# Retention and routed experts on one core: logits one chunk further behind, expert 0's weights loaded later and evenly, and a third list for expert 0

## The chip, the core and the metric

The kernel runs on one core of a Trainium2 chip. Its engines are TensorE (PE, with its weight loads shown apart as PEld), VectorE (DVE), ScalarE (ACT), GpSimd (POOL) and SyncE (SP); each takes its own instructions in the order in which they are written. SP issues most transfers, POOL the gathers and scatters, and 16 DMA engines carry them all. TensorE's clock is granted at one of two levels, 1.2 or 2.4 GHz (0.50 and 1.00 in the rows). The metric is the time of one execution on the device in microseconds (us), the median of several.

## The reference

Four sequences of 768 tokens with 8 heads of 64 run through a linear attention with decay ("retention"); its output, 3072 tokens of 512 numbers, goes through a layer of 8 experts of which each token uses the two with the largest noisy logits.

```python
for t in range(S):
    state = gamma[None, :, None, None] * state + np.einsum('bhd,bhe->bhde', k[:, :, t], v[:, :, t])
    y[:, :, t] = scale * np.einsum('bhd,bhde->bhe', q[:, :, t], state)
...
logits = x @ w_gate
noise_scale = np.log1p(np.exp(x @ w_noise))
noisy_logits = logits + noise_scale * noise
top2 = np.argpartition(-noisy_logits, 2, axis=1)[:, :2]
...
h = np.maximum(x[mask] @ w1[e], 0.0)
out[mask] += top2_w[mask, k, None] * (h @ w2[e])
```

## The kernel before

**Retention** goes through 24 chunks of 128 tokens, six to a sequence. `qk(j)` makes chunk j's first product (16 matmuls, L306, always the first of its chunk in the trace) and DVE masks it into `am` (L309). `y_mm(j)` makes the chunk's output `pY` (L316, L320) and, except in a sequence's last chunk, the state's increment `pU` (L324), which ACT copies into `U` (L330) for the next chunk's L316; the first chunk of a sequence reads no `U`. Then ACT squares `pY` for its norm (L333), DVE makes the scale (`x_scale`, L152 to L155), ACT makes `xs` and its float16 half (L342, L343), POOL the rest (L344), and SP sends the result twice: transposed to `xt` for the logits (L346) and to `xbuf` in memory for the experts (L347). `logits(j)` (L353, L356) are 8 small matmuls on `xt`.

The loop at L633 writes these in a fixed order. Iteration j holds `qk(j+1)`, the scaling of v and q on POOL, `x_scale(j-1)` and `x_split(j-1)`, the loads of chunk j+4, `y_mm(j)`, the logits of an earlier chunk, and then what a table `todo[j]` names. So on DVE an iteration is the mask of chunk j+1, the scale of chunk j-1 and the table's work; on ACT `xs` and its half come before `U`.

**Routing** of a sequence b is such table work, in steps: `route_a` (logits out of PSUM), `route_b` (the two largest, one-hot), `route_c` (exponential on ACT, weights; on PE the places in the lists, L404 and L407), `route_h`, `route_d` (places), `route_e` twice (one-hot matrices `ob`, `a`, `bb`, L468 to L478), `route_f` (12 matmuls, L485, added to `acc`), `route_g`. The tuple `when` gives the iteration of each, counted from the sequence's last chunk.

**Experts.** A token list per expert is packed into blocks of 128 slots. Expert 0 is worked on first, and its first 384 slots (list 0, the first two sequences) already while the last sequence is routed: `units` are eight `mm1` (first product of 384 slots, L672 to L674, 12 matmuls each) and three `mm2` (second product of a block, L702 to L704), and `early(n)` puts n of them into PE's order. Its other tokens (list 8) begin at slot 384 or later. `slots` reads a block's tokens from `acc`, `gather` fetches them (POOL, L591), `x_t` transposes them into `xe` (SP, L598), `put` scatters the result (POOL, L693). The weights of expert 0 come in quarters by `w_load` (SP, L171), `w_sum` (ACT, L175), `w_hi` (ACT, L192) and `w_lo` (DVE, L197), from the same table; those of expert 1 are loaded after the ranking of the experts, and the rest follow one expert ahead. The order after the loop is written out by hand:

```python
    early(1)
    logits(NCH - 3)
...
    early(1)
    logits(NCH - 2)
...
    early(1)
    logits(NCH - 1)
    route_a(b)
    route_b(b)
```

Of the kernel before, what the change touches and what calls it, by code (L numbers as in the profile page):

```python
# [32 lines left out]
# fullest with the most slots.  What exceeds an expert's slots goes through the loop at the end.  # L33
B0 = B // 2
FIRST = 384
NL = E + 1
NBLK, CAP = 7, 832
CAPS = [832, 832, 816, 800, 800, 784, 768, 768]      # expert 0, then by rank
NCOL = NBLK * E
BASE = [NBLK * 128 * e for e in range(E)] + [0]  # L40
NV = 5
BIG = 1.0e6
# powers of two that the float16 parts are scaled to (bounds of the norms)
# [4 lines left out]
for _n, _w in (("ident", 128), ("mask", 128), ("tri", 128), ("lanes", 128), ("blks", NCOL),  # L48
               ("lidx", NL), ("base", NL), ("rcap", E - 1), ("tie", E - 1), ("tok1", NCH), ("tokv", NCH * 2), ("pad", 1), ("i64", 64),
               ("vtab", NC * H), ("gtab", NC * HP)):  # L50
    _C[_n] = (_o, _o + _w)
    _o += _w
# [4 lines left out]
def _constants():  # L57
# [11 lines left out]
    put("lidx", np.arange(NL)[None, :])  # L69
    put("base", np.array(BASE)[None, :])  # L70
# [21 lines left out]
def moe_kernel(ctx, tc, qT, kT, kt, vt, noise, wgn, w1, w2, ctab, qtab, xbuf, out):  # L92
# [9 lines left out]
    # keeps the tensor engine's clock up while the first operands come in  # L102
# [28 lines left out]
    idx = consts.tile([128, NCOL], I32, name="idx")            # by rank  # L131
# [12 lines left out]
    LST = pR[:, 160:160 + NV * NCOL].rearrange("p (v n) -> p v n", v=NV)  # L144
    SUM = pR[:, 480:488]

    def pow2(ss, target, up, down):
        """Power of two that brings a vector with sum of squares ss below 2^target, and its inverse."""
        # sqrt(ss) < 2^(m - 62) with m half the biased exponent of ss; powers of two by their bits
# [13 lines left out]
    def w_load(e, which, i, n=1):  # L163
        # n quarters from the ith on
# [44 lines left out]
    # ================= retention and routing =================  # L209
# [33 lines left out]
    def zero_out(i):  # L243
        # the output and the rows of padding start as zeros
# [44 lines left out]
    def q_table(c):  # L289
        # the decay of chunk c's queries, out of chunk 0's  # L290
# [84 lines left out]
    def route_b(b):  # L375
        # noisy logits, the two largest
        lg, sp = R[b]
        o = int(b >= B0)
        ny = work.tile([128, NC, NL], F32, name="ny")
        nc.vector.tensor_tensor(sp, sp, nz[:, b * NC:(b + 1) * NC, :], op=OP.mult)  # L380
        nc.vector.memset(ny[:, :, 0:1] if o else ny[:, :, E:NL], -3.0e38)
# [9 lines left out]
        for k in range(2):  # L391
            nc.vector.tensor_tensor(oh[:, k], K("lidx")[:, None, :].to_broadcast(s3),
                                    i8[:, :, k:k + 1].to_broadcast(s3), op=OP.is_equal)
# [6 lines left out]
    def route_c(b):  # L400
        # places in the lists
# [14 lines left out]
        # what the slots get: token + 1 in two parts, the weight in three, each exact in bfloat16  # L416
# [15 lines left out]
    def route_d(b):  # L432
# [11 lines left out]
        if b == B0 - 1:  # L444
            nc.vector.tensor_scalar(cn[:, E:NL], cn[:, 0:1], float(FIRST), None, op0=OP.max)
# [14 lines left out]
    def route_e(b, k):  # L460
        # the slots' tokens and weights as sums of one-hot products
# [10 lines left out]
        # the last sequence's are waited for: GpSimd takes a part  # L472
# [21 lines left out]
    def slots(n0, n1):  # L494
        # token + 1 and weight, 0 in empty slots
# [6 lines left out]
    def rows_of(tk, n0, n1):  # L502
        # the slots' rows in xbuf and out; a row of padding for an empty slot
# [4 lines left out]
    def ranks():  # L508
        # experts 1, ..., 7 by their tokens' number
# [8 lines left out]
        pm = hp.tile(s3, F32, name="pm")           # rank by expert  # L518
# [15 lines left out]
    def route_g(b):  # L534
        # what the loop over the places beyond the lists needs
# [10 lines left out]
    def loop_table():  # L546
        # blocks beyond the lists: how many, of which list, from which place
# [38 lines left out]
    def gather(e, t):  # L586
        o, n, i = block(e, t)
        if t == 0:
# [3 lines left out]
            out=x[:n], out_offset=None, in_=xbuf[:128 + B0 * S] if e == 0 and t < 3 else xbuf,  # L592
# [347 lines left out]
```

## Time and profile before

| | |
|---|---|
| median of 3 runs | 724.33 us (724.18 to 725.54) |
| profiled execution, first to last instruction | 733.5 us |
| TensorE busy | 685.0 us, 93% of the span |
| VectorE, ScalarE, GpSimd busy | 294.0, 311.0, 237.9 us |
| mean granted TensorE clock | 0.954 |

The page gives no time of the profiled execution but its span; that is 9.2 us above the median of the runs without a profile. PE's busy time is no measure of speed where the clock is at half, since the same matmul is then busy for longer.

### The profile page before, as it was taken

What the parts mean: (1) busy time and instruction counts of PE and PEld (TensorE: products, weight loads), DVE (VectorE), ACT (ScalarE), POOL (GpSimd) and SP (SyncE); (2) the same over time, 40 slices, a digit from 0 to 9 for tenths busy, and PEclk for the clock granted to TensorE, in tenths of its full rate; (3) what the DMA queues carried; (4) which work ended last, traced back from release to release, by engine and by line L of the source; (5) the groups of instructions that cost most, each with busy time, mean ns of one, the idle gap of its engine ahead of it and who ended that gap; (6) DMA issues with size and microseconds to landing.
All of it is one profiled execution on the core that took longest, in us unless ns stands there. A gap on an engine that the chain in (4) does not pass through costs nothing.

```text
span 733.5 us, 12009 instructions
## 1 busy us (share of the span) xinstructions
PE 685.0 (93%) x4789; PEld 431.0 (59%) x4789; DVE 294.0 (40%) x719; ACT 311.0 (42%) x562; POOL 237.9 (32%) x186
## 2 busy tenths in 40 slices
PE   8879879889879999999999999999999999999991
PEld 6879769777448555455546545654555466446540
DVE  3326778695942573215221521432152225216100
ACT  4554444447204374344443534443444435344110
POOL 4564734652333220431033123304321421240021
PEclk9997787986999999999999999999999999999997
DMA  9999955995869953467367826744673685353032
GB/s 331 260 296 245 290 181 165 294 294 146 303 115 248 216 163 130 88 115 221 84 115 120 267 45 119 182 155 86 116 218 85 122 177 185 68 104 60 11 47 30
DMA packets 116057, 119.09 MB, mean 162 GB/s; under 512 B 82560, under 2 KB 82816, under 8 KB 112416
## 3 DMA queue, kind: packets, MB, share of 16 engines
q1 hardware_dynamic: 104080, 91.25, 45.0%
q0 software_dynamic: 11344, 26.22, 19.4%
q10 hardware_dynamic: 576, 0.84, 0.4%
q8 instruction: 38, 0.62, 0.4%
q14 instruction: 19, 0.16, 0.1%
HBM read 72.67 MB, written 26.21 MB: 135 GB/s over the span
## 4 chain that ended last, share of the span: by engine, by line
PE 76%; DVE 8%; DMA 7%; ACT 3%; issue 2%; POOL 1%; SPq 1%; POOLq 0%; ACTq 0%
PE pH L672 11%; PE pH L673 11%; PE pH L674 11%; PE pO L702 10%; PE pO L704 10%; PE pO L703 10%; PE pY L320 3%; DMA xt<-x 3%; PE pA L306 2%; PE pY L316 2%; PE pU L324 1%; DMA wst<-w 1%; DVE am L309 1%; DVE bb L478 1%; DMA xe<-xg 1%
## 5 line engine op out<-in xcount | busy, mean ns | idle before, releaser
L693 POOL DMA_INDIRECT out<-ot,idx x54 | 84.9, 1573 | 360.2 <-ACT ot L688 214.4
L672 PE MATMUL pH<-xe,w1h 128*128 128x384 f16 (+4 forms) x544 | 176.6, 325 | 3.9 <-DMA xe<-xg 3.3
L673 PE MATMUL pH<-xe,w1h 128*128 128x384 f16 (+4 forms) x544 | 176.5, 324 | 0.0
L674 PE MATMUL pH<-xe,w1l 128*128 128x384 f16 (+4 forms) x544 | 176.4, 324 | 0.0
L676 DVE SCALAR_TENSOR_TENSOR hl<-pH,hh 128x384 f16<-128x384 f32 (+4 forms) x136 | 74.4, 549 | 210.5 <-ACT hh L675 209.7
L704 PE MATMUL pO<-w2h,hl 128*128 128x512 f16 x384 | 145.5, 379 | 0.0
L703 PE MATMUL pO<-w2l,hh 128*128 128x512 f16 x384 | 145.5, 379 | 0.0
L702 PE MATMUL pO<-w2h,hh 128*128 128x512 f16 x384 | 145.5, 379 | 0.0
L675 ACT ACTIVATE hh<-pH 128x384 f16<-128x384 f32 (+4 forms) x136 | 65.7, 483 | 127.1 <-PE pH L674 125.2
L688 ACT ACTIVATE ot<-pO,gse 128x512 f32<-128x512 f32 (+4 forms) x54 | 37.0, 686 | 173.8 <-PE pO L704 169.3
L197 DVE SCALAR_TENSOR_TENSOR w1l<-wst,wsc,w1h 128x1024 f16<-128x1024 f32 x32 | 42.7, 1339 | 106.8 <-ACT w1h L192 106.8
L672 PEld LDWEIGHTS <-w1h 128*128 128x128 f16 x544 | 54.2, 100 | 34.5 <-DMA xe<-xg 1.7
L673 PEld LDWEIGHTS <-w1h 128*128 128x128 f16 x544 | 53.5, 98 | 35.4 <-issue 2.8
L674 PEld LDWEIGHTS <-w1l 128*128 128x128 f16 x544 | 53.5, 98 | 34.5 <-issue 0.3
L175 ACT ACTIVATE junk<-wst 128x1024 bf16<-128x1024 f32 x64 | 67.1, 1049 | 5.6 <-DMA wst<-w 2.8
L704 PEld LDWEIGHTS <-hl 128*128 128x128 f16 x384 | 37.5, 98 | 45.8 <-DVE hl L676 0.5
L702 PEld LDWEIGHTS <-hh 128*128 128x128 f16 x384 | 38.1, 99 | 44.1
L703 PEld LDWEIGHTS <-hh 128*128 128x128 f16 x384 | 37.5, 98 | 44.2
L591 POOL DMA_INDIRECT xg<-xbuf,idx x54 | 54.7, 1014 | 25.9 <-issue 14.9
L320 PE MATMUL pY<-vp,am 128*128 128x64 f32 x384 | 60.4, 292 | 0.0
L320 PEld LDWEIGHTS pY<-vp,am 128*128 128x128 f32 x384 | 58.1, 220 | 0.6 <-issue 0.2
L344 POOL TENSOR_TENSOR x<-xs,x 128x512 f16<-128x512 f32 x23 | 32.3, 1405 | 58.6 <-issue 32.3
(163 smaller groups left out, 778.1 us busy)
## 6 DMA issues: line engine op xcount, KB each, us to landing
wst<-w SPq DMA_DIRECT2D x28, 1024.0 KB, 9.2
in_q<-qT SPq DMA_DIRECT2D x24, 256.0 KB, 3.7
in_k<-kT SPq DMA_DIRECT2D x24, 256.0 KB, 4.2
in_v<-vt SPq DMA_DIRECT2D x24, 256.0 KB, 4.9
in_kt<-kt SPq DMA_DIRECT2D x24, 256.0 KB, 5.0
xbuf<-x SPq DMA_DIRECT2D x24, 256.0 KB, 2.6
out<-zero SPq DMA_DIRECT2D x6, 1024.0 KB, 12.6
wst<-w SPq DMA_DIRECT2D x8, 512.0 KB, 7.6
```

Of the source, the lines that this page charges most:

```text
L175: nc.scalar.activation(junk, st[:, i * 1024:(i + 1) * 1024], AF.Square, accum_out=ss[:, i:i + 1])
L320: nc.tensor.matmul(pY[:, 2 * i + s, :], AM[j][:, s, i, :], VP[j][:, 2 * i + s, :], start=(not c and i == 0 and s == 0), stop=True, skip_gr ...
L591: nc.gpsimd.indirect_dma_start(out=x[:n], out_offset=None, in_=xbuf[:128 + B0 * S] if e == 0 and t < 3 else xbuf, in_offset=bass.IndirectO ...
L672: nc.tensor.matmul(p[:, :n], whi, xh, start=(k == 0), stop=False)
L673: nc.tensor.matmul(p[:, :n], whi, xl, start=False, stop=False)
L674: nc.tensor.matmul(p[:, :n], wlo, xh, start=False, stop=(k == KT - 1))
L675: nc.scalar.activation(hh[:, f, n0:n1], p[:, :n], AF.Relu)
L676: nc.vector.scalar_tensor_tensor(hl[:, f, n0:n1], p[:, :n], 0.0, hh[:, f, n0:n1], op0=OP.max, op1=OP.subtract)
L693: nc.gpsimd.indirect_dma_start(out=out, out_offset=bass.IndirectOffsetOnAxis(ap=idx[:n, i:i + 1], axis=0), in_=ot[:n], in_offset=None, com ...
L702: nc.tensor.matmul(p, a, WT["2h"][:, f, :], start=(f == 0), stop=False)
L703: nc.tensor.matmul(p, a, WT["2l"][:, f, :], start=False, stop=False)
L704: nc.tensor.matmul(p, c, WT["2h"][:, f, :], start=False, stop=(f == FT - 1))
```

## The change

Five things change; all else, the experts 1 to 7 included, is written in the same order.

1. `logits` stand three chunks behind instead of two, and `when` is moved with them: `route_b` and `route_c` no longer share an iteration, but `route_c` and `route_h` do, and so do `route_d` and the first `route_e`.
2. Expert 0's weights start two iterations later (w1) and are spread over every second iteration (w1 in 5 to 11, w2 in 13 to 19; before 3 to 9 and 17 to 20).
3. The third sequence's `route_f` moves from the last iteration to behind the first early unit; its second `route_e` moves into the last iteration.
4. The fourth sequence's tokens of expert 0 get a list of their own (list 9 of 10) that begins at slot 576 or later. So slots 384 to 575 are ready once the third sequence is routed: `units` gain eight `mm1` of 192 slots and a fourth `mm2`. Of the block that is cut at 576 the two halves are gathered and transposed apart.
5. `route_g` of the last two sequences and the loop's table move from expert 0's second product to expert 1's.

```diff
-    LST = pR[:, 160:160 + NV * NCOL].rearrange("p (v n) -> p v n", v=NV)
+    LST = pR[:, 168:168 + NV * NCOL].rearrange("p (v n) -> p v n", v=NV)
...
-            nc.vector.tensor_tensor(oh[:, k], K("lidx")[:, None, :].to_broadcast(s3),
+            nc.vector.tensor_tensor(oh[:, k], K("lidx3" if b == B - 1 else "lidx")[:, None, :].to_broadcast(s3),
...
-            nc.vector.tensor_scalar(cn[:, E:NL], cn[:, 0:1], float(FIRST), None, op0=OP.max)
+            nc.vector.tensor_scalar(cn[:, E:E + 1], cn[:, 0:1], float(FIRST), None, op0=OP.max)
+        if b == B - 2:
+            nc.vector.tensor_scalar(cn[:, E + 1:NL], cn[:, E:E + 1], float(SECOND), None, op0=OP.max)
...
-        when = (1, 2, 2, 3, 3, 4, 5, 6, 7) if b < B - 2 else (1, 2, 2, 3, 3, 3, 4, 5)
+        when = (2, 3, 4, 4, 5, 5, 6, 7, 7) if b < B - 2 else (2, 3, 4, 4, 4, 4, 5)
...
-        at(3 + 2 * i, w_load, 0, "1", i)
-        at(5 + 2 * i, w_sum, 0, "1", i)
...
+        at(5 + 2 * i, w_load, 0, "1", i)
+        at(7 + 2 * i, w_sum, 0, "1", i)
+        at((14, 15, 17, 18)[i], w_hi, 0, "1", i)
+        at((15, 16, 18, 19)[i], w_lo, 0, "1", i)
+        at(13 + 2 * i, w_load, 0, "2", i)
+        at((15, 17, 19, 21)[i], w_sum, 0, "2", i)
...
-        if 2 <= j < NCH - 1:
-            logits(j - 2)
+        if j >= 3:
+            logits(j - 3)
...
+    units += [lambda f=f: mm1(0, FIRST, SECOND, f) for f in range(FT)]
+    units += [lambda t=t: first.append(mm2(0, t)) for t in range(3, mid)]
...
     early(1)
+    route_f(b - 1)
+    slots(3, mid + 1)
+    for t in range(3, mid + 1):
+        gather(0, t, 0, min(128, SECOND - t * 128), (B - 1) * S)
+    for t in range(3, mid + 1):
+        x_t(0, t)
     logits(NCH - 3)
...
-    for t in range(3):
+    for t in range(mid):
         put(0, t, first[t])
...
-        cols = [(FIRST, 640), (640, CAPS[0])] if e == 0 else [(0, half), (half, CAPS[e])]
+        cols = [(SECOND, CAPS[0])] if e == 0 else [(0, half), (half, CAPS[e])]
...
-            if e == 0 and n == 2:
+            if e == 1 and n == 2:
                 route_g(b - 1)
```

On DVE in iteration 9 of the kernel before, the last of `route_d` for the first sequence (`lb`, `lf`) is followed by the mask and the scale of the next iteration, and only then by the first `route_e`:

```order
L454 TENSOR_SCALAR lb<-si 128x12
L455 TENSOR_SCALAR lb<-si 128x12
L457 CAST lf<-lb 128x24
L309 TENSOR_TENSOR am<-pA,ct 128x512 x2
L152 TENSOR_SCALAR p2m<-xss 128x1
L153 TENSOR_SCALAR xsc<-p2m 128x1
L155 TENSOR_SCALAR invx<-p2m 128x1
L468 TENSOR_TENSOR ob<-blks,lf 128x336
```

The same place of the change, iteration 11 (its lines are numbered 3 to 5 higher):

```order
L459 TENSOR_SCALAR lb<-si 128x12
L460 TENSOR_SCALAR lb<-si 128x12
L462 CAST lf<-lb 128x24
L473 TENSOR_TENSOR ob<-blks,lf 128x336
L475 TENSOR_TENSOR a<-lanes,lf 128x768
L483 TENSOR_TENSOR bb<-ob,vv 128x1680
L312 TENSOR_TENSOR am<-pA,ct 128x512 x2
L155 TENSOR_SCALAR p2m<-xss 128x1
L156 TENSOR_SCALAR xsc<-p2m 128x1
```

The mask `am` and the scale `xsc` of the next iteration now stand behind `ob`, `a` and `bb` as well.

On DVE behind the last chunk, from its `x` (chunk 23) to the copy of the last sequence's logits `lg`, the kernel before has:

```order
L344 TENSOR_TENSOR x_2069<-xs,x_2069 128x512
L197 SCALAR_TENSOR_TENSOR w2l<-wst_1590,wsc_1592,w2h 128x1024
L490 TENSOR_TENSOR acc<-acc,pR 128x280
L197 SCALAR_TENSOR_TENSOR w2l<-wst_1590,wsc_1592,w2h 128x1024
L676 SCALAR_TENSOR_TENSOR hl<-pH,hh 128x384 x3
L366 COPY lg<-pL 128x96
```

and the change:

```order
L347 TENSOR_TENSOR x_2067<-xs,x_2067 128x512
L200 SCALAR_TENSOR_TENSOR w2l<-wst_1219,wsc_1221,w2h 128x1024
L473 TENSOR_TENSOR ob<-blks,lf 128x336
L475 TENSOR_TENSOR a<-lanes,lf 128x768
L483 TENSOR_TENSOR bb<-ob,vv 128x1680
L200 SCALAR_TENSOR_TENSOR w2l<-wst_1219,wsc_1221,w2h 128x1024
L684 SCALAR_TENSOR_TENSOR hl<-pH,hh 128x384
L495 TENSOR_TENSOR acc<-acc,pR 128x280
L501 TENSOR_TENSOR tk<-acc 128x2
L510 TENSOR_SCALAR padv<-tk,ct 128x2
L511 SCALAR_TENSOR_TENSOR idx<-tk,padv 128x2
```

The third sequence's second `ob`, `a`, `bb` moved behind the last chunk's `x`, and the sum `acc` with the slots that it gives behind the first unit's `hl`.

On PE the third sequence's 12 list matmuls (L485, in the change L490) follow the last chunk's output in the kernel before:

```order
L316 MATMUL pY<-U_161,qs 128x128
L320 MATMUL pY<-vp,am 128x64 x2
L485 LDWEIGHTS a
L485 MATMUL pR<-bb,a 128x280
```

and in the change the first early unit:

```order
L681 LDWEIGHTS w1h
L681 MATMUL pH<-xe,w1h 128x384
L682 LDWEIGHTS w1l
L682 MATMUL pH<-xe,w1l 128x384
L490 LDWEIGHTS a
```

So one early unit moved ahead of the list matmuls; the logits of the last three chunks and all other units stand behind them in both.

## Rows read from the trace of the kernel before

**Rows 1.** Busy time by stretch: us, busy of PE, PEld, DVE, ACT, POOL, PEclk, DMA, GB/s
```profile
23.66:54.39 30.73, 24.15 (x268) 22.63 (x264) 7.91 (x25) 17.01 (x39) 19.21 (x17) 1.00 1.10 292
54.39:99.41 45.02, 41.38 (x346) 38.44 (x342) 29.61 (x96) 19.07 (x41) 23.08 (x17) 0.73 0.89 254
99.41:144.22 44.81, 36.50 (x343) 33.91 (x340) 35.39 (x97) 20.31 (x43) 25.04 (x19) 0.85 0.75 217
144.22:157.63 13.41, 10.76 (x123) 10.02 (x120) 12.62 (x51) 5.68 (x16) 9.61 (x9) 1.00 1.06 330
...
221.60:723.40 501.80, 495.64 (x3220) 272.67 (x3218) 156.37 (x287) 213.66 (x352) 129.50 (x99) 1.00 0.57 130
```
**Rows 2.** What PE waited for from 20 to 224 us; last, from 23.66 to 54.39: us, times, longest
```profile
PE pL L353 <- DMA xt<-x: 12.4, 10, 2.5
PE pR L404 <- DVE mb L395: 6.5, 2, 5.1
PE pY L316 <- ACT U L330: 4.3, 4, 1.4
PE pH L672 <- DMA xe<-xg: 3.3, 1, 3.3
...
PE pL L353 <- DMA xt<-x: 5.3, 4, 2.5
```
**Rows 3.** PE in order of time: two first products, and a wait for U
```profile
18.62 1.16 PE L306 MATMUL pA<-qs,in_k 64*128 64x128 f32 x16
23.66 1.16 PE L306 MATMUL pA<-qs,in_k 64*128 64x128 f32 x16
...
76.71 0.49 PE L316 MATMUL pY<-U,qs 128*128 128x128 f32 x2 [0.79 <-ACT U L330]
```
**Rows 4.** Stretches at half clock: us, PE busy, PEclk, DMA share, GB/s
```profile
54.36:64.60 10.24, 10.24 (x74) 0.50 1.14 308
...
160.17:177.24 17.07, 15.68 (x78) 0.50 0.58 131
218.20:221.61 3.41, 3.41 (x19) 0.50 0.44 46
```
**Rows 5.** DVE in order of time, the first sequence's routing
```profile
65.24 0.79 DVE L411 TENSOR_SCALAR dn<-den 128x6 f32<-128x6 f32 x1 [3.95 <-ACT den L403]
...
68.09 0.18 DVE L427 CAST vv<-g 128x12 bf16<-128x12 f32 x1
...
73.03 1.27 DVE L309 TENSOR_TENSOR am<-pA,ct 128x512 f32<-128x512 f32 x2
...
74.53 0.50 DVE L468 TENSOR_TENSOR ob<-blks,lf 128x336 bf16<-128x336 bf16 x1
...
77.64 1.28 DVE L309 TENSOR_TENSOR am<-pA,ct 128x512 f32<-128x512 f32 x2
```
**Rows 6.** ACT in order of time: U behind xs and its half, then the norm
```profile
74.65 0.69 ACT L342 ACTIVATE xs<-pY,xsc 128x512 f32<-128x512 f32 x1 [2.54 <-DVE xsc L153]
...
75.90 0.75 ACT L330 ACTIVATE U<-pU 64x256 f32<-64x256 f32 x2
76.68 0.60 ACT L333 ACTIVATE junk<-pY 128x512 bf16<-128x512 f32 x1
```
**Rows 7.** PE and DVE in order of time, the end of the retention
```profile
173.52 3.01 PE L485 MATMUL pR<-bb,a 128*128 128x280 bf16 x12
...
177.34 1.28 DVE L197 SCALAR_TENSOR_TENSOR w2l<-wst,wsc,w2h 128x1024 f16<-128x1024 f32 x1 [0.29 <-ACT w2h L192]
...
183.03 0.18 PE L353 MATMUL pL<-wg,xt 128*128 128x32 f16 x1
```
**Rows 8.** POOL, SP and ACT in order of time: last early put, expert 1's w2
```profile
223.56 1.56 POOL L693 DMA_INDIRECT out<-ot,idx  x1 [3.90 <-ACT hh L675]
...
238.05 1.32 SPq L171 DMA_DIRECT2D wst<-w  x2
...
256.48 1.05 ACT L175 ACTIVATE junk<-wst 128x1024 bf16<-128x1024 f32 x1
```

More of the change, by code (lines that the diff above doesn't have):

```diff
@@ L34 @@
 B0 = B // 2
-FIRST = 384
-NL = E + 1
+FIRST, SECOND = 384, 576
+NL = E + 2
+NY = E + 1
 NBLK, CAP = 7, 832
@@ L39 @@
 NCOL = NBLK * E
-BASE = [NBLK * 128 * e for e in range(E)] + [0]
+BASE = [NBLK * 128 * e for e in range(E)] + [0, 0]
 NV = 5
@@ L48 @@
 for _n, _w in (("ident", 128), ("mask", 128), ("tri", 128), ("lanes", 128), ("blks", NCOL),
-               ("lidx", NL), ("base", NL), ("rcap", E - 1), ("tie", E - 1), ("tok1", NCH), ("tokv", NCH * 2), ("pad", 1), ("i64", 64),
+               ("lidx", NL), ("lidx3", NL), ("base", NL), ("rcap", E - 1), ("tie", E - 1), ("tok1", NCH), ("tokv", NCH * 2), ("pad", 1), ("i64", 64),
                ("vtab", NC * H), ("gtab", NC * HP)):
@@ L69, in _constants @@
     put("lidx", np.arange(NL)[None, :])
+    put("lidx3", np.array(list(range(E)) + [NL, E])[None, :])
     put("base", np.array(BASE)[None, :])
@@ L378, in route_b @@
         o = int(b >= B0)
-        ny = work.tile([128, NC, NL], F32, name="ny")
+        ny = work.tile([128, NC, NY], F32, name="ny")
         nc.vector.tensor_tensor(sp, sp, nz[:, b * NC:(b + 1) * NC, :], op=OP.mult)
-        nc.vector.memset(ny[:, :, 0:1] if o else ny[:, :, E:NL], -3.0e38)
+        nc.vector.memset(ny[:, :, 0:1] if o else ny[:, :, E:NY], -3.0e38)
         nc.vector.tensor_tensor(ny[:, :, o:o + E], sp, lg[:, :, :E], op=OP.add)
@@ L568, in loop_table @@
         le = work.tile([128, 64], F32, name="le")
-        nc.vector.tensor_scalar(loop_e, loop_e, float(E), None, op0=OP.min)
-        nc.vector.tensor_scalar(le, loop_e, float(E), -float(E), op0=OP.is_equal, op1=OP.mult)
-        nc.vector.tensor_tensor(loop_i[:, :64], loop_e, le, op=OP.add)
+        nc.vector.tensor_scalar(loop_e, loop_e, float(NL - 1), None, op0=OP.min)
+        nc.vector.tensor_scalar(le, loop_e, float(E), None, op0=OP.is_lt)
+        nc.vector.tensor_tensor(loop_i[:, :64], loop_e, le, op=OP.mult)
         nc.vector.tensor_copy(loop_i[:, 64:65], cs[:, NL - 1:NL])
@@ L584, in blocks, with gather @@
         return range(-(-CAPS[e] // 128))
-    def gather(e, t):
+    def gather(e, t, p0=0, p1=128, rows=N):
         o, n, i = block(e, t)
+        p1 = min(n, p1)
         if t == 0:
@@ L591, in gather @@
         nc.gpsimd.indirect_dma_start(
-            out=x[:n], out_offset=None, in_=xbuf[:128 + B0 * S] if e == 0 and t < 3 else xbuf,
-            in_offset=bass.IndirectOffsetOnAxis(ap=idx[:n, i:i + 1], axis=0))
-        XG[e, t] = x
+            out=x[:p1], out_offset=None, in_=xbuf[:128 + rows],
+            in_offset=bass.IndirectOffsetOnAxis(ap=idx[:p1, i:i + 1], axis=0))
+        XG[e, t] = x, o, p0, p1
     def x_t(e, t):
-        o, n, i = block(e, t)
-        nc.sync.dma_start_transpose(XE[e][:, :, o:o + n], XG.pop((e, t))[:n])
+        x, o, p0, p1 = XG.pop((e, t))
+        nc.sync.dma_start_transpose(XE[e][:, :, o + p0:o + p1], x[p0:p1])
     steps = (route_a, route_b, route_c, route_h, route_d, route_e, route_e, route_f, route_g)
     for b in range(B - 1):
-        when = (1, 2, 2, 3, 3, 4, 5, 6, 7) if b < B - 2 else (1, 2, 2, 3, 3, 3, 4, 5)
+        when = (2, 3, 4, 4, 5, 5, 6, 7, 7) if b < B - 2 else (2, 3, 4, 4, 4, 4, 5)
         k = 0
@@ L612, in moe_kernel @@
     for i in range(4):
-        at(3 + 2 * i, w_load, 0, "1", i)
-        at(5 + 2 * i, w_sum, 0, "1", i)
-        at((12, 13, 14, 15)[i], w_hi, 0, "1", i)
-        at((13, 14, 15, 17)[i], w_lo, 0, "1", i)
-        at(17 + i, w_load, 0, "2", i)
-        at((18, 19, 21, 21)[i], w_sum, 0, "2", i)
+        at(5 + 2 * i, w_load, 0, "1", i)
[4 more added lines that the diff above has]
+        at((15, 17, 19, 21)[i], w_sum, 0, "2", i)
     at(2, nc.vector.tensor_copy, lanes, K("lanes"))
     at(2, nc.vector.tensor_copy, blks, K("blks"))
-    todo[12].insert(0, (w_scale, (0, "1")))
+    todo[14].insert(0, (w_scale, (0, "1")))
     at(NCH - 2, w_scale, 0, "2")
-    at(NC * (B0 + 1) + 1, slots, 0, 3)
+    at(NC * (B0 + 1) + 2, slots, 0, 3)
     for t in range(3):
-        at(NC * (B0 + 1) + 1 + t // 2, gather, 0, t)
-        at(NC * (B0 + 1) + 2 + t // 2, x_t, 0, t)
+        at(NC * (B0 + 1) + 2 + t // 2, gather, 0, t, 0, 128, B0 * S)
+        at(NC * (B0 + 1) + 3 + t // 2, x_t, 0, t)
+    mid = SECOND // 128
     at(1, nc.sync.dma_start, xbuf[:128, :], zero.bitcast(F16))
@@ L748, in moe_kernel @@
     route_b(b)
-    out_scale(0, 0, 3)
+    out_scale(0, 0, mid)
     early(3)
@@ L759, in moe_kernel @@
     route_f(b)
-    slots(3, NBLK)
-    for t in range(3, NBLK):
-        gather(0, t)
+    slots(mid, NBLK)
+    for t in range(mid, NBLK):
+        gather(0, t, SECOND - t * 128 if t == mid else 0)
         x_t(0, t)
@@ L766, in moe_kernel @@
     ranks()
-    out_scale(0, 3, NBLK)
-    for t in range(3):
+    out_scale(0, mid, NBLK)
+    for t in range(mid):
         put(0, t, first[t])
@@ L801, in moe_kernel @@
                     w_sum(e + 1, "1", n - (len(cols) * FT - 5))
-                if e == 0 and n >= 12:
+                if e == 0 and n >= 4:
                     ahead.pop(0)()
@@ L809, in moe_kernel @@
                 w_scale(e + 1, "1")
-        todo = list(range(3, NBLK)) if e == 0 else list(blocks(e))
+        todo = list(range(mid, NBLK)) if e == 0 else list(blocks(e))
         for n, t in enumerate(todo):
```

## Prediction

> **What bounds the kernel now.** I read the busy time by stretch first, then PE's waits, then the chain of waits through the retention engine by engine. From 221.6 to 723.4 us PE is busy for 495.6 of 501.8 us at full clock [rows 1]; the change leaves that work as it is. What can move lies before. A chunk of the retention without a wait takes 5.04 us from first product to first product [rows 3]. Chunks 4 to 8 (23.66 to 54.39) took 30.7 us where five such take 25.2; chunks 9 to 14 took 45.0 and 15 to 20 took 44.8 where six take 30.2; 21 and 22 took 13.4 instead of 10.1 [rows 1]. Two things fill the difference. PE waits for `xt` (12.4 us), for the one-hot `mb` (6.5) and for `U` (4.3) [rows 2]. And the granted clock falls to 0.50, 1.2 GHz, after such waits: five stretches from 54.36 to 177.24, 54.6 us together, of which the rows show the first and the last [rows 4]; each microsecond of them costs half a microsecond if PE sets the pace, 27 us at most.
>
> The `xt` waits are a matter of order: the transfer is done soon after, so another chunk of distance covers it. Behind them stands DVE. In the first sequence's routing it reached the mask 2.6 us late, at 73.03 us, because `route_h` and `route_d` (68.09 to 73.03, 4.9 us) stood ahead; the scale came after the mask, ACT made `xs`, its half and then `U` by 76.65, and PE began at 76.71 [rows 5, 6, 3]. PE lost only 0.79 us: about 1.1 us of lateness is free, and more goes to PE almost in full.
>
> **The change part by part**, each from the profiled execution's 733.5 us; the median of the runs shown is 9.2 us less, and I carry the difference over to it unchanged.
>
> *Chunks 4 to 8.* No routing runs here. Four of the ten waits for `xt` lie in this stretch, 5.3 of the 12.4 us [rows 2]. DMA engines are at 1.10 with 292 GB/s [rows 1], so part may come back as a wait for loads: 0 to -5.3, and as one quarter of w1 leaves the stretch I take **-4.5**. The Trainium skill ("DMA: Bandwidth & Descriptors", Where 436 GB/s comes from) gives some 358 GB/s to one core's traffic with HBM: by that figure, an estimate, the 9.0 MB of this stretch need 25 us, no more than PE does, and the term would be -5.3. The busy share of 1.10 says that the engines had little left at 292; another row of this trace reaches 330.
>
> *Chunks 9 to 14, first sequence's routing.* The waits for `xt` and `mb` go. What comes is DVE's clump. Count from the end Q of the first product in the iteration that now holds `route_c` and `route_h`. That pair needs an exponential on ACT that stands behind `U` and the norm, and DVE sits until then, as it did for 3.95 us [rows 5]: PE's other work of the chunk ends at Q+3.7, `U` takes 0.75, norm and exponential about 1 [rows 3, 6], so DVE begins at Q+5.5. `route_c` with the next iteration's mask and scale takes 2.85 (65.24 to 68.09), `route_h` and `route_d` 4.9, and the first `route_e`, now without a mask between, 3.1 (74.53 to 77.64) [rows 5]: 16.4. Mask and scale 1.5 (73.03 to 74.53): 17.9. `xs`, its half and `U` 2.0 (74.65 to 76.65) [rows 6]: Q+19.9. PE without waits would want that `U` at Q+13.4, since the sequence's last chunk between is short. So PE stalls for 6.5 us, first at a product whose PSUM buffer the late mask holds, then for `U`. Waits of 2.5 us and less brought the clock down before; with the mean stretch of 54.6/5 = 10.9 us it costs 5.4. 30.2 + 6.5 + 5.4 = 42.1 against 45.0: **-2.9**. Bounds: -12 if DVE's lateness and the clock cost nothing, 0 if half clock lasts the longest stretch, 17.07 us [rows 4].
>
> *Chunks 15 to 20, second sequence.* The same clump, with four `w_lo` of 1.3 us or more [rows 7] among it: two of them and the longer `route_b` iteration come ahead of the decisive mask, and the same count ends 4.5 us later, a stall of 11. 30.2 + 11 + 5.4 = 46.6, less 0.5 that DVE catches up while PE is slow, against 44.8: **+1.3** (bounds -9 to +5).
>
> *Chunks 21 and 22*: one routing step each; 10.4 against 13.4, **-3.0**. The sum so far is -9.1: the first product of chunk 23 starts at 148.5 instead of 157.63.
>
> *The end of the retention.* Here the change adds a wait. On PE the third sequence's 12 list matmuls stood behind the last output at 173.52 and needed nothing late [rows 7]. They now stand behind the first unit and need the second `bb`, which on DVE follows the last chunk's `x` and a `w_lo`. From the end Q of chunk 23's first product: exponential Q+5.5; `route_c`, `h`, `d` and the first `route_e` on DVE 9.4 by [rows 5]; two scales 0.9; `xs` and half 1.3 and norm 0.8 on ACT [rows 6]; scale, `xs`, half and `x` of the last chunk 2.3; `w_lo` 1.3 [rows 7]; `ob`, `a`, `bb` 3.1: about Q+24.5. PE has finished its unit at about Q+9.5, so it sits for some 15 us and falls to half clock. Behind the list matmuls wait logits 21 to 23 and two units. Before, the list matmuls and three units took 9.5 us to the last logits at 183.03 [rows 7]; with a unit less, at half clock, about 8: Q+32.5. Before it was Q+24.2, Q being 157.63 + 1.16. The last sequence's whole routing waits for these logits: **+8.5** (bounds +3, if the exponential's wait vanishes and `route_e` is quick, to +12).
>
> *Expert 0's third list.* After the last `route_f` PE had two `mm2`, then waited 3.3 us for `xe` [rows 2] and ran 3.41 us at half clock, 1.7 lost [rows 4]. Now eight `mm1` of 192 slots and an `mm2`, 13 us that were done later before, stand there and cover both: **-5.0**. Total PE work is the same. The zeroing of the output moves behind two more gathers and transposes on SP; the 13 us also cover that. The reference's own draw (its seed 0) fills expert 0 up to slot 741 before and 746 now, of 832, so the loop gets no block.
>
> *Expert 1.* A fourth `put` stands ahead of its gathers on POOL; the third took 5.5 us with its wait [rows 8]. So expert 1's tokens and the w2 load behind them on SP (238.05) come some 5 us later, while ACT wants w2 (256.48) 5 us earlier [rows 8]: of 18 us for landing and slack 8 are left. The 2.1 MB need 8.4 us at 250 GB/s, and the stretches show 130 to 330 [rows 1]: 0 to +3, I take **+1**. DVE's wider rows (60 elements for 54) and the moved table, which lies beside some 20 us of `mm2`, add too little to count.
>
> Sum: -4.5 - 2.9 + 1.3 - 3.0 + 8.5 - 5.0 + 1.0 = **-4.6 us**: 728.9 of 733.5, and 719.7 of 724.33.
>
> **The rivals.** *The clump hides* (18%). For it: 2.6 us of lateness cost 0.79 [rows 3, 5], and DVE sits idle while it waits for ACT. Against: no row shows DVE late by more than that without PE standing. With both stalls halved, 3.3 + 5.5 us go: 710.9; less where the clock stays up too.
>
> *The waits come back as waits for loads* (13%), so the change does not do what it says: if DMA has no more to give in chunks 4 to 8, the -4.5 is 0, and the rest sums to nothing: 724.2.
>
> *The clock stays down* (27%), which makes it slower. Place: after the two stalls in chunks 9 to 20. At half clock PE was busy for 15.7 of 17.07 us and yet was not granted more [rows 4]. I count 22 us at half clock in these chunks; each further one costs 0.5, so from 31 us on the change loses. Before, 37.7 lay there (clock 0.73 over 45.02 and 0.85 over 44.81 us [rows 1]). At 45, two stretches of the longest kind and one of the mean, the time is 731. The Trainium skill ("TensorE: Matmul & The Clock Gate", HAM oscillation) says that a wait between groups of matmuls is paid again as cold matmuls behind it; the trace agrees, and by that rule alone every new stall here speaks against the change.
>
> **How the numbers follow.** The likeliest case (42%) is the sum, with 714 to 722.8 as its own range. No change is within 0.2%, 1.4 us, about what three runs can tell. Faster: 0.42 + 0.18 = 0.60; same 0.13; slower 0.27. Below 707 only the hiding case with the clock up reaches (7%), above 731 the clock staying down for longest or the end at its bound (12%).
>
> **What would show it.** Right: no wait for `xt` or `mb` in the retention; a wait of PE for `bb` of about 15 us ahead of the list matmuls, behind one unit; PE standing for `U` and for a masked buffer in chunks 13 and 19, some 6 and 11 us, each followed by half clock; chunk 23 starting near 148; no wait for `xe` of expert 0, full clock there. Wrong: chunk 23 before 140 or after 156; a wait for `bb` under 6 us; PE waiting for `w1l` or ACT for `wst` at expert 1.

## The result, and the profile after

The changed kernel takes 733.05 us (median of 20 runs, 728.11 to 738.30); the kernel before, run beside it, takes 725.09 (20 runs, 721.23 to 731.19). The ratio, by which every run below is compared, is 1.0088, interval 1.0065 to 1.0112: 6.4 us slower (the two medians are 8.0 us apart), where 4.6 us less were forecast.

The page of the profiled execution, span and busy time:

```profile
span 731.6 us, 12030 instructions
...
PE 681.4 (93%) x4789; PEld 426.5 (58%) x4789; DVE 293.4 (40%) x726; ACT 311.6 (43%) x562; POOL 234.3 (32%) x187
```

This span is that of a run of 733.43 us, near the median. Beside the span of 733.5 from which the prediction was made, the change would seem to have gained 1.9 us. But that execution of before was slower than every one of its 20 runs here; so the comparison of the two profiles misleads, and the medians decide.

Busy time by stretch, with the stretches of [rows 1], the end of the retention (chunk 23's first product to its logits) and the half-clock stretches that answer to [rows 4]:

```profile
23.34:48.60 25.26, 23.53 (x265) 22.60 (x264) 7.91 (x25) 15.03 (x36) 17.21 (x16) 1.00 1.07 294
48.60:91.75 43.15, 36.21 (x339) 33.59 (x339) 28.56 (x86) 21.35 (x48) 25.27 (x21) 0.84 1.03 307
91.75:137.43 45.68, 40.61 (x342) 38.28 (x341) 35.16 (x100) 22.64 (x48) 21.70 (x18) 0.74 0.84 241
137.43:149.97 12.54, 10.23 (x113) 9.78 (x112) 11.41 (x47) 7.35 (x17) 6.47 (x7) 1.00 0.86 237
149.97:179.95 29.98, 20.86 (x162) 16.37 (x162) 19.16 (x59) 13.82 (x23) 8.55 (x8) 0.83 0.58 123
...
77.62:91.27 13.65, 11.33 (x63) 10.28 (x64) 6.84 (x14) 5.93 (x13) 7.88 (x6) 0.50 0.84 250
111.75:135.65 23.90, 20.42 (x115) 19.20 (x115) 20.86 (x44) 9.09 (x16) 11.06 (x8) 0.50 0.73 200
159.54:166.37 6.83, 6.83 (x38) 5.72 (x38) 4.63 (x15) 1.89 (x4) 0.61 (x1) 0.50 0.40 93
...
200.50:203.91 3.41, 3.41 (x10) 1.22 (x9) 1.16 (x6) 0.00 (x0) 1.80 (x2) 0.50 0.30 86
261.94:265.35 3.41, 3.41 (x11) 1.52 (x10) 1.73 (x8) 1.08 (x2) 1.45 (x1) 0.50 0.28 59
```

What PE waited for, from 20 to 224 us as in [rows 2], and then from 224 to 300 us, where the kernel before had no wait:

```profile
PE pR L490 <- DVE bb L483: 7.7, 2, 5.4
PE pA L309 <- POOL qs L289: 5.9, 6, 1.9
PE pY L319 <- ACT U L333: 5.5, 5, 1.6
PE pA L309 <- DVE am L312: 4.2, 3, 1.9
PE pR L182 <- DVE cum L446: 3.7, 1, 3.7
...
PE pR L182 <- ACT junk L178: 3.0, 1, 3.0
PE pH L680 <- DVE hl L684: 1.0, 2, 0.6
```

The waits for `xt`, `mb` and `xe` are gone, as forecast, and so is the whole difference of chunks 4 to 8 to full pace (five chunks of 5.04 us are 25.2). The wait for `bb` ahead of the last logits is there. What the prediction put at 0 to +3 us is the last pair: PE stands at expert 1. PE in order of time at these places:

```profile
79.06 2.07 PE L309 MATMUL pA<-qs,in_k 64*128 64x128 f32 x14 [1.88 <-DVE am L312]
82.01 0.80 PE L319 MATMUL pY<-U,qs 128*128 128x128 f32 x2 [0.87 <-ACT U L333]
...
158.95 0.35 PE L182 MATMUL pR<-wss,onef 128*128 128x4 f32 x2 [3.69 <-DVE cum L446]
...
173.53 1.56 PE L490 MATMUL pR<-bb,a 128*128 128x280 bf16 x6 [5.43 <-DVE bb L483]
...
259.87 0.39 PE L182 MATMUL pR<-wss,onef 128*128 128x4 f32 x2 [3.00 <-ACT junk L178]
260.90 0.34 PE L680 MATMUL pH<-xe,w1h 128*128 128x416 f16 x1 [0.64 <-DVE hl L684]
```

The wait at 259.87 can be followed back through four engines. DVE, SP, POOL and ACT in order of time (`eid` is the ranking of the experts, which SP reads before it can load expert 1's weights):

```profile
200.43 0.45 DVE L495 TENSOR_TENSOR acc<-acc,pR 128x280 f32<-128x280 f32 x1 [0.98 <-PE pR L490]
...
220.76 0.36 DVE L684 SCALAR_TENSOR_TENSOR hl<-pH,hh 128x192 f16<-128x192 f32 x1 [0.63 <-ACT hh L683]
...
222.92 0.17 DVE L528 CAST eid<-rk 128x7 int32<-128x7 f32 x1
...
227.54 0.94 SPq L174 DMA_DIRECT2D wst<-w  x2
...
228.41 1.02 POOL L598 DMA_INDIRECT xg<-xbuf,idx  x1 [0.31 <-issue]
...
238.66 5.42 SPq L605 DMA_TRANSPOSE xe<-xg  x4
244.34 1.30 SPq L174 DMA_DIRECT2D wst<-w  x2
...
257.49 1.06 ACT L178 ACTIVATE junk<-wst 128x1024 bf16<-128x1024 f32 x1 [2.87 <-DMA wst<-w]
```

From the bottom: PE waits for the sum of squares that ACT makes of w2; ACT waits for w2's transfer, issued at 244.34; SP could not issue it sooner, because four transposes stand ahead and waited until 238.66 for expert 1's gathered tokens; the first of the gathers, issued at 228.41, took 10.2 us to land, and w1's load began 0.9 us ahead of it; and w1's load waited for the ranking, which comes 22.5 us after the last sum `acc` (3.2 us after it in the kernel before, 206.74 behind 203.55), because the `hl` of the third list's eight units stand ahead of it on DVE.

The same places in the kernel before, where PE did not wait:

```profile
206.74 0.41 DVE L523 CAST eid<-rk 128x7 int32<-128x7 f32 x1
208.90 7.36 SPq L598 DMA_TRANSPOSE xe<-xg  x4
221.59 0.93 SPq L171 DMA_DIRECT2D wst<-w  x2
225.43 1.02 POOL L591 DMA_INDIRECT xg<-xbuf,idx  x1 [0.30 <-DVE hl L676]
232.24 5.55 SPq L598 DMA_TRANSPOSE xe<-xg  x4
```

There the ranking was done before expert 0's transposes, SP came to w1's load 5.3 us behind them, the gathers began 3.8 us after that, and the first landed in 6.8 us. So on SP the load moved by 6 us, not by the 16 us of the ranking.

### The profile page after: what moved, and what is told of

Read it like the earlier page. It is cut to its first block, busy times and chain, and to the rows that moved or that the text cites. A ratio compares the mean times of both kernels' runs of the same rounds, so it can differ in the third digit from the quotient of the medians.

```text
span 731.6 us, 12030 instructions
## 1 busy us (share of the span) xinstructions
PE 681.4 (93%) x4789; PEld 426.5 (58%) x4789; DVE 293.4 (40%) x726; ACT 311.6 (43%) x562; POOL 234.3 (32%) x187
## 4 chain that ended last, share of the span: by engine, by line
PE 72%; DVE 12%; DMA 6%; ACT 4%; issue 3%; SPq 2%; POOL 1%; POOLq 0%; DVEq 0%; ACTq 0%
PE pH L680 11%; PE pH L682 10%; PE pH L681 10%; PE pO L712 10%; PE pO L711 10%; PE pO L710 10%; PE pY L323 2%; DVE am L312 2%; DVE bb L483 2%; DMA wst<-w 2%; PE pY L319 2%; DMA xg<-xbuf,idx 1%; DMA out<-ot,idx 1%; PE pU L327 1%; PE pA L309 1%
## 5 line engine op out<-in xcount | busy, mean ns | idle before, releaser
L701 POOL DMA_INDIRECT out<-ot,idx x54 | 86.3, 1599 | 356.9 <-ACT ot L696 220.4
L598 POOL DMA_INDIRECT xg<-xbuf,idx x55 | 56.5, 1028 | 38.4 <-issue 15.4
L712 PEld LDWEIGHTS <-hl 128*128 128x128 f16 x384 | 37.6, 98 | 46.4 <-DVE hl L684 0.9
L711 PEld LDWEIGHTS <-hh 128*128 128x128 f16 x384 | 37.7, 98 | 44.4 <-issue 0.8
L347 POOL TENSOR_TENSOR x<-xs,x 128x512 f16<-128x512 f32 x23 | 29.2, 1270 | 55.3 <-ACT x L346 22.2
```

Source lines behind the costliest of these rows:

```text
L598: nc.gpsimd.indirect_dma_start(out=x[:p1], out_offset=None, in_=xbuf[:128 + rows], in_offset=bass.IndirectOffsetOnAxis(ap=idx[:p1, i:i + 1 ...
L701: nc.gpsimd.indirect_dma_start(out=out, out_offset=bass.IndirectOffsetOnAxis(ap=idx[:n, i:i + 1], axis=0), in_=ot[:n], in_offset=None, com ...
L711: nc.tensor.matmul(p, a, WT["2l"][:, f, :], start=False, stop=False)
L712: nc.tensor.matmul(p, c, WT["2h"][:, f, :], start=False, stop=(f == FT - 1))
```

## The experiments

Each run is compared with the kernel before, run beside it on the same chip. Ratios are to its time; microseconds are the ratio's distance from 1 times the median of before there (727 to 732 us).

**The kernel before, again**, with no edit.

> The kernel before, unchanged, profiled a second time. Theory M: the profiled execution on which the prediction was worked out (733.5 us from first to last instruction, with the runs at 721 to 731 us) was an untypically slow one, and what it had too much lies in the retention, at half clock. Then this execution spans some 723 us, chunk 23's first product starts near 149 instead of 157.63, and less than 35 us of the first 225 are at half clock, where there were 58. Rival R: that execution was typical, and the loss is what the change adds. Then the span is near 733 and chunk 23 starts near 157. The ratio is 1.000 by both.

Ratio 0.9985 (0.9953 to 1.0017); span 730.3 in a run of 732.1, its median here. Its stretches:

```profile
23.61:56.02 32.41, 28.12 (x269) 26.88 (x265) 7.91 (x25) 15.79 (x36) 17.90 (x16) 0.84 1.06 305
56.02:96.80 40.78, 35.60 (x345) 33.33 (x342) 29.34 (x96) 20.65 (x45) 24.59 (x19) 0.87 0.91 258
96.80:140.67 43.87, 35.37 (x342) 33.23 (x339) 36.50 (x97) 19.04 (x41) 24.47 (x18) 0.88 0.72 206
140.67:157.64 16.97, 10.69 (x124) 9.95 (x120) 14.36 (x62) 8.51 (x21) 10.40 (x10) 1.00 1.07 330
157.64:178.62 20.98, 18.97 (x149) 15.71 (x147) 14.96 (x30) 14.72 (x26) 5.53 (x4) 0.84 0.81 146
```

Chunk 23 starts where it did, so M fell for the chunks. Up to there 30.7 us are at half clock where the first profile had 37.5, and yet chunk 23 is no earlier. But the end of the retention takes 21.0 us where the first profile had 25.4, and from 195 to 224 us PE waits for `bb` alone: the 3.3 us for `xe` that the third list was to take away are not there.

**Order alone, weights alone, list alone.** Each is the kernel before with one part of the diff: `when` and `logits` with `route_f(b - 1)` behind the first early unit; the weights' table; the third list.

```diff
# order
+        when = (2, 3, 4, 4, 5, 5, 6, 7, 7) if b < B - 2 else (2, 3, 4, 4, 4, 4, 5)
+        if j >= 3:
+            logits(j - 3)
# weights
+        at(5 + 2 * i, w_load, 0, "1", i)
+        at(13 + 2 * i, w_load, 0, "2", i)
# list
+    units += [lambda f=f: mm1(0, FIRST, SECOND, f) for f in range(FT)]
+    units += [lambda t=t: first.append(mm2(0, t)) for t in range(3, mid)]
```

> Of the change only the order: logits three chunks behind, the routing steps moved with them, the third sequence's list matmuls behind the first early unit. The weights' table and expert 0's lists are those of before. Theory M (the routing's clumps cost no more than the stalls they replace; PE waits for the list matmuls ahead of the last logits): +2 to +5 us, of which the wait for bb behind the first early unit is 5; expert 1 does not wait. Rival R (the clumps on VectorE between chunks 9 and 20 are the loss): +7 us or more, with chunk 23's first product 5 us or more later than in the kernel before of the same call.

> Of the change only the table of expert 0's weights, two iterations later and spread evenly; all else as before. Theory M: within 2 us of before, since the logits two chunks behind still wait for their transposed tokens and the transfers in chunks 4 to 8 only become a quarter less. Rival R (the loads of weights bound chunks 4 to 8, and their move is worth something by itself): -3 us or more.

> Of the change only the third list of expert 0, with its 8 first products of 192 slots and fourth second product ahead of the last list matmuls; logits, routing steps and weights stand as before. Theory M (the list takes away the wait for the gathered tokens, 5 us, but the ranking of the experts and with it expert 1's loads come 6 us later while PE needs them 6 us earlier, so that PE stands at expert 1): +1 us, between -1 and +3, with a wait of PE of 3 us or more for the sum of squares of w2 in expert 1's first product. Rival R (expert 1's wait costs nothing that was not waited before): -4 us.

Order: 1.0083 (1.0052 to 1.0114), +6.1 us; between M and R. Chunk 23 starts at 153.6, 4 us earlier than in the kernel before again and not later, as R asked; the last logits come 34.2 us behind it instead of 21.0, so the loss lies at the end of the retention. Weights: 0.9921 (0.9892 to 0.9950), -5.8 us; R's size, but not its place: chunks 4 to 8 take 30.5 us, no less than in other profiles of the retention of before (29.0 to 34.0), so what the weights' table gains is not explained. List: 1.0070 (1.0031 to 1.0109), +5.1 us; worse than either theory, with 1.0 us of waiting for w2 in a profile that was the fastest of its twelve runs. The three together are +5.4 us, about the change's loss.

**Order and weights together**, without the list:

> Order and weights together, without the third list. By the prediction's terms for chunks 4 to 22 and the end of the retention it is -0.6 us, by the two single runs +0.3 us: ratio 0.998 to 1.002 (theory M: the loss of the change is the list's). Rival R (order and weights act on each other, and the loss is in them): ratio 1.005 or more.

1.0018 (0.9985 to 1.0051): neutral, M. So the list added to order and weights makes the change's loss. This is one way to divide it: the order alone costs as much, and only the weights' gain covers it. List and weights without the order were not run.

**Expert 1 earlier, in the changed kernel and in the kernel before.** The ranking and the loads of expert 1's w1 and w2 move ahead of the remaining units:

```diff
-    early(len(units))
     slots(NBLK, NCOL)
     ranks()
...
+    for which in ("1", "2"):
+        w_load(1, which, 0, 2)
+        w_load(1, which, 2, 2)
+    early(len(units))
```

> The changed kernel with one thing moved: the ranking of the experts and the loads of expert 1's w1 and w2 stand ahead of expert 0's remaining early units instead of behind them. Theory M (with the third list the loads of expert 1 come some 6 us later on SP while TensorE wants them 6 us sooner; the profile after shows 3.0 us of waiting for the sum of squares of w2, 0.6 for hl and 3.4 us at half clock there): 5 us less than the change, a ratio to before near 1.002, no wait of TensorE at expert 1. Rival R (the wait only moves to expert 1's gathered tokens or its w1): ratio stays at 1.007 or more.

> The kernel before with the ranking of the experts and the loads of expert 1 ahead of the remaining early units, the same move that took 7 us from the changed kernel. Theory M (the kernel before does not wait there; the wait was made by the third list): ratio within 0.3% of 1. Rival R (the move is worth the same to any version, so that it says nothing on the list): ratio 0.992 or less.

The changed kernel goes from 1.0088 to 0.9993 (0.9962 to 1.0024), with no wait of PE from 205 to 300 us; the kernel before stays at 1.0005 (0.9964 to 1.0046). M on both: the list made the wait. The same move on the list alone:

> The third list alone (logits, routing steps and weights as before) with the ranking of the experts and expert 1's loads ahead of the remaining early units. Theory M (the list alone lost 5 us only because the loads of expert 1 stand behind its units): ratio between 0.994 and 1.001, no wait at expert 1. Rival R (the list costs by itself: a fourth scatter on GpSimd, wider rows on VectorE, two more gathers): ratio 1.005 or more still.

0.9948 (0.9915 to 0.9981), M: with the loads early the list is worth something. The list alone a second time:

> The third list alone, a second time: the profile of the first was the fastest of its twelve executions and showed 1.0 us of waiting at expert 1. Theory M: the other executions wait there for w2's sum of squares or for tokens, 3 us or more, and this profile, if it is of a slower execution, shows it. Rival R: the slower executions differ in the retention alone, and expert 1 waits 1 us or less here too.

1.0070 (1.0032 to 1.0109) again. The profile, of a typical run (737.9 us), shows 1.8 us for w2's sum and 0.6 for `hl` at expert 1: less than M asked. Its span is 8.2 us longer than that of the first profile, but 7.7 of them fall before the last list matmul (206.5 against 198.8); from there to expert 2 both take the same (119.7 and 119.6 us). So what makes this execution slow lies in the retention and the routing, as R said, though not within R's 1 us at expert 1. From the last list matmul to expert 2 it is 3.8 us longer than with the loads early, so the profiles show less than half of the 8.9 us (1.2%) between these two kernels; where the rest falls stays open.

**Which link of the chain.** The changed kernel with only the ranking and w1's load early, and with only w2's load moved, to right behind w1's:

```diff
# ranking
     w_load(1, "1", 2, 2)
+    early(len(units))
# w2
     w_load(1, "1", 2, 2)
+    w_load(1, "2", 0, 2)
+    w_load(1, "2", 2, 2)
```

> The changed kernel with only the ranking of the experts and w1's load for expert 1 ahead of the remaining early units; w2's load stays behind expert 1's first four transposes. Theory M1 (the chain starts at the ranking: it stands behind eight new units on VectorE, so that w1's transfer begins a microsecond ahead of the gathers and makes them land late, and w2 behind them): w1 has landed before the gathers start, they land in 7 us instead of 10, and most of the 7 us come back, ratio 1.000 to 1.004. Rival M2 (the place of w2's load behind the transposes decides, since the fourth scatter delays the gathers anyway): ratio 1.006 or more, with a wait for w2's sum of squares.

> The changed kernel with only w2's load for expert 1 moved, from behind its first four transposes to right behind w1's load; the ranking stays behind the units. Theory M1 (the ranking is the start of the chain): w2 no longer waits, but w1 and w2 together stand in front of the gathers, expert 1's tokens land later still and TensorE waits for them or for w1; ratio 1.006 or more. Rival M2 (w2's place decides): ratio 1.000 to 1.003, no wait at expert 1.

The first: 1.0028 (1.0004 to 1.0051), no wait at expert 1. Its DVE, SP and POOL:

```profile
205.63 0.42 DVE L528 CAST eid<-rk 128x7 int32<-128x7 f32 x1
...
217.34 0.93 SPq L174 DMA_DIRECT2D wst<-w  x2
...
230.39 1.02 POOL L598 DMA_INDIRECT xg<-xbuf,idx  x1 [0.30 <-issue]
...
234.72 6.55 SPq L605 DMA_TRANSPOSE xe<-xg  x4
241.53 1.08 SPq L174 DMA_DIRECT2D wst<-w  x2
```

The gathers start 2.0 us later than in the change, yet the transposes behind them 3.9 us earlier: the first landed in 4.3 us instead of 10.2, with w1's load 13 us ahead of it. The second: 1.0115 (1.0063 to 1.0166), PE now waits 2.2 us for expert 1's tokens. M1 on both: the place of the ranking, with w1's load behind it, decides, not w2's.

**The list matmuls behind the last logits, the steps apart, and all three moves.** The first moves `route_f(b - 1)` with its slots and gathers behind `route_b(b)`; the second is

```diff
-        when = (2, 3, 4, 4, 5, 5, 6, 7, 7) if b
+        when = (2, 3, 4, 5, 5, 6, 7, 8, 8) if b
```

> The changed kernel with one thing moved: the third sequence's list matmuls, its slots and their gathers stand behind the last logits and the first two routing steps of the last sequence instead of behind the first early unit. Theory M (TensorE stands for bb ahead of the last three logits): 5 to 6 us less than the change, ratio near 1.001, last logits some 23 us behind the first product of chunk 23 where the change has 30. Rival R (VectorE is late with x of the last chunk as well, so the logits wait for their tokens instead, or the list's gathers come too late for its units): ratio 1.006 or more.

> The changed kernel with the routing steps of the first two sequences in iterations 2, 3, 4, 5, 5, 6, 7, 8, 8 instead of 2, 3, 4, 4, 5, 5, 6, 7, 7, so that places and first one-hot matrices share no iteration; the third sequence as in the change. Theory M (two clumps on VectorE make TensorE stand in chunks 13 and 19, and each brings half clock): 4 us less than the change, ratio near 1.003; chunks 9 to 20 in 85 us or less where the change takes 88.8. Rival R (VectorE's work per iteration only moves, and the later steps collide with the next sequence's first): no less than the change.

> The changed kernel with all three moves of the runs of this call. Theory M: the three add up, 14 us less than the change, ratio near 0.99. Rival R (they share one wait, that of the last sequence's routing, so that only the largest counts): ratio near 1.001.

The list matmuls: 1.0115 (1.0062 to 1.0169), R's ratio. Last logits come 27.2 us behind chunk 23 instead of 30.0, and PE then waits 5.1 us for expert 1's tokens: the gain was lost there. The steps apart: 0.9972 (0.9936 to 1.0009), 8 us less than the change; chunks 9 to 20 take 78.6 us instead of 88.8. M: the clumps had a price. All three: 0.9974 (0.9936 to 1.0011), neither theory. Last logits are 8 us earlier than with the steps apart alone, but PE stands 6.7 us at expert 1, with this on POOL (L701 scatters expert 0's early blocks, L598 gathers for expert 1):

```profile
207.01 1.62 POOL L701 DMA_INDIRECT out<-ot,idx  x1 [9.00 <-ACT hh L683]
213.78 1.57 POOL L701 DMA_INDIRECT out<-ot,idx  x1 [5.15 <-DMA out<-ot,idx]
224.13 1.57 POOL L701 DMA_INDIRECT out<-ot,idx  x1 [8.78 <-DMA out<-ot,idx]
230.34 1.56 POOL L701 DMA_INDIRECT out<-ot,idx  x1 [4.64 <-DMA out<-ot,idx]
232.21 1.03 POOL L598 DMA_INDIRECT xg<-xbuf,idx  x1 [0.30 <-issue]
```

The second to fourth scatter each wait for the one before to land, and the gathers stand behind all four. **With the gathers ahead** of the scatters (and, on SP, w2's load behind their transposes instead of ahead of them):

```diff
     w_load(1, "1", 2, 2)
+    for t in range(4):
+        gather(1, t)
+        x_t(1, t)
```

> The kernel of the run with all three moves, with one more: on GpSimd the gathers of expert 1's first four blocks, and on SP their transposes, stand ahead of expert 0's four early scatters instead of behind them. Theory M (with all three moves TensorE stood 6.7 us for expert 1's tokens, because the four scatters wait for each other's landing and the gathers stand behind them; that is where the three moves' gain went): no such wait, 6 to 9 us less, ratio near 0.987. Rival R (the transfers themselves are late, since w1, w2 and the zeroing take the queues at that time): the wait stays, under other names, ratio 0.995 or more.

0.9897 (0.9849 to 0.9945), 717.5 us beside 726.6: M, the best kernel here, faster than the kernel before and the change. From 205 to 300 us PE waits for nothing. The edit moves gathers and w2's load together; which of the two does it was not run apart.

**Logits that catch up**, three behind to iteration 18 and two from 19 on, with the third sequence's steps and `route_f` as before, steps apart, expert 1 early and gathers ahead:

```diff
+        if 3 <= j < 20:
+            logits(j - 3)
+        if 19 <= j < NCH - 1:
+            logits(j - 2)
```

> The changed kernel with expert 1's ranking, loads and first gathers early, the first two sequences' routing steps apart, and logits that catch up: three chunks behind up to iteration 18, two behind from iteration 19, so that the third sequence's routing and its list matmuls stand where the kernel before has them. Theory M (logits three behind are worth their gain in the chunks, and cost it again only at the end, where the third sequence's one-hot matrices come late ahead of the last logits): chunk 23's first product near 144, last logits 21 us later as in the kernel before, span near 717, ratio near 0.982. Rival R (VectorE's work from chunk 18 on is what binds, wherever the steps stand): last logits 26 us or more behind chunk 23, ratio 0.99 or more.

0.9943 (0.9911 to 0.9975): a gain, but not M's, and less than that of the run before. Chunk 23 starts at 148.5 where it was 143.2 there, with a wait of 5.8 us for `mb` back on PE; the last logits come 23.0 us later instead of 26.0. What is saved at the end is paid in the chunks.

**The change again**:

> The changed kernel, unchanged, on this chip. All theories: ratio near 1.009; by theory M the end of the retention takes 28 us or more from chunk 23's first product to the last logits, and TensorE waits 2 us or more for the sum of squares of w2 in expert 1.

1.0150 (1.0090 to 1.0209). The profile, of the fastest of four runs (728.1 us), has the same retention (last logits 30.1 us behind chunk 23) and, against M, no wait for w2:

```profile
227.04 0.93 SPq L174 DMA_DIRECT2D wst<-w  x2
227.91 1.03 POOL L598 DMA_INDIRECT xg<-xbuf,idx  x1 [0.30 <-issue]
238.15 5.41 SPq L605 DMA_TRANSPOSE xe<-xg  x4
243.83 0.99 SPq L174 DMA_DIRECT2D wst<-w  x2
253.90 1.06 ACT L178 ACTIVATE junk<-wst 128x1024 bf16<-128x1024 f32 x1 [1.67 <-DMA wst<-w]
```

The late ranking, w1's load 0.9 us ahead of the gathers and their 10.2 us are all there again. What differs is w2's own transfer: 10.0 us (243.83 to 253.8) where it took 13.1. So the late chain brings w2 near to its limit in both executions, and the length of one transfer decides whether PE waits; why that varies is not shown.

## Why the prediction was wrong

**The terms, measured.** Six profiled executions have the retention of before (its two, the list's two, and those of before and of the list with the loads early), five that of the change (its two, and those with expert 1 early, with the ranking early and with w2 ahead). Lengths between first products (the last: to the last logits), means in us:

```
                 before (range)       change (range)       moved   predicted
chunks 4-8       31.4 (29.0-34.0)     25.5 (24.6-26.5)     -5.9    -4.5
chunks 9-14      40.2 (36.2-45.0)     42.6 (41.6-43.2)     +2.3    -2.9
chunks 15-20     43.9 (43.0-44.8)     46.1 (44.8-47.0)     +2.3    +1.3
chunks 21-22     17.2 (13.4-21.3)     12.6 (12.5-12.6)     -4.6    -3.0
end              21.4 (17.7-25.4)     31.9 (30.0-33.9)    +10.5    +8.5
sum                                                        +4.6    -0.6
```

The chips differ, so the sum is rough; the run of order and weights together says +1.3 us (-1.1 to +3.7). Each sign but one was right, and this half of the prediction comes out within 2 to 5 us.

**The step that failed** is the pair "Expert 0's third list: -5.0" and "Expert 1: +1", together -4. Measured alone the list is +5.1 us, 9 off, which is most of the miss of 11. Two things that the prediction itself named as signs of being wrong came: ACT waited for `wst` at expert 1 (2.87 us), and PE waited less than 6 us for `bb`. The step failed twice.

The gain was sized from one execution. Of the 3.3 us for `xe` and the half clock behind it, five further profiles without the list or with only parts of the change show 0, 0, 2.0, 3.1 and 0.5 us, and none the half clock. In the change the wait for `xe` is gone, but the full clock that was forecast there is not: 3.41 us are at half clock from 200.50 on.

The loss was priced on half of its chain. I followed the fourth scatter to the gathers and to w2, and had w2's load come 5 us later; it came 6.3 us later (244.34 for 238.05). But only 3.0 us of that are the gathers' later start (228.41 for 225.43); the rest is that the first of them took 10.2 us to land instead of 6.8, with w1's load 0.9 us ahead of it instead of 3.8. That link was missing: `ranks` stands behind `early(len(units))` in both kernels, adding eight units put their `hl` ahead of it on DVE, and w1's load moved from 221.59 to 227.54, into the gathers. With the ranking and w1's load ahead of the units, the ratio falls from 1.0088 to 1.0028. The slack of 8 us that I left for w2 also took a transfer of 8.4 us for granted; it took 13.1 (244.34 to 257.4). PE's wait of 3.6 us and 1.7 us lost at half clock (3.41 at 0.50) are 5.3 where I put 1.

The profiles side by side agree in sign. From the last list matmul to expert 2's first product, five without the list and with the ranking where it was take 117.3 to 121.3 us (118.6 on the mean; both of before, order, weights, and these two together), five with the list and the ranking behind its units 119.1 to 123.9 (121.1; both of the change, both of the list, and the steps apart), and three with the list and the ranking ahead 115.7 to 115.9. So the list costs 2.5 us there with a late ranking and gives 2.8 with an early one. By the runs it is +5.1 and -3.8 us (0.9948); the rest is not located by any profile.

**The base.** The prediction carried over the distance of 9.2 us between the profiled execution and the median as if it were a constant. It was chance: chunks 9 to 14 and the end took 45.0 and 25.4 us there, the longest of six executions, and it is from there that the -2.9 came. Against the mean of six the same clumps are +2.3.

**The clumps** were right as a mechanism (undoing them gave 8 us) and wrong inside. I forecast stalls of 6.5 and 11 us with 10.9 us at half clock behind each. PE stood 2.8 us in iteration 13 (1.88 and 0.87), and from 60 to 137 us it waited 11.3 us in all, spread over nine waits of 1.9 us at most, of which three (3.5 us) were for POOL's `qs`, which the prediction had nowhere; but the half clock lasted 13.65 and 23.90 us. Too much stall and too little half clock cancelled in the sum: that the two terms gave 88.2 us for chunks 9 to 20 and the profile 88.8 is luck. (The 1.1 us of lateness called free does not follow from the figures beside it: 2.6 less 0.79 is 1.8. The sum does not use it.) So the rival "the clock stays down" was right about the clock, 37.6 us at half clock in these chunks, above its point of 31 (the kernel before had 37.7 there), but not about its price, since the stalls were shorter.

**The end of the retention**: the wait for `bb` was 5.4 us, not 15. DVE had `bb` done at Q+22.4 instead of Q+24.5, since `route_h` and `route_d` took 2.8 us instead of the 4.9 of [rows 5]; and PE, which was to be through its unit at Q+9.5, came to the list matmuls only at Q+16.1, behind a wait of 3.7 us that I had not seen (its small matmul for w2's scale, L182, stands behind the third sequence's `cum`) and 6.83 us at half clock from 159.54 on. Logits came at Q+28.8 in this profile instead of Q+32.5, but the base was Q+20 on the mean, not Q+24.2; the term of +8.5 (8.3 by its own two figures) came out as +10.5.

## What to carry to other kernels

Work that is put in front of a common "finish the rest" call also moves everything written behind that call, on every engine: follow each of them, not only the one that the work was meant to help. A wait that one profiled execution shows is worth its size only if other executions have it; profile the base twice before a gain of 1% is priced. And a gain before a chain of scatters and gathers reaches the end only if that chain starts earlier too.

## What was unexpected

The same program varies by over 1% from run to run (721.2 to 731.2 us), and the retention of before by 14 us from chip to chip and run to run (last logits at 169.2 to 183.0 us), while that of the change varies by 8 (179.5 to 187.8). The half-clock stretches fall elsewhere each time; in the second profile of before one lies in the middle of the experts (519.8 to 523.2 us), where PE had waited for 0.5 us at most at a time. The first of expert 1's gathers took 4.3 us to land with w1's load 13 us ahead of it, 6.8 us with it 3.8 us ahead, and 10.2 us with it 0.9 us ahead.
